# Eight shared PSUM banks, diagonal score blocks of their own, and two copies moved to ScalarE

## The chip, the core and the metric

The kernel runs on one core of a Trainium2 chip. The metric is the device time of one execution in microseconds (us), the median of several runs. The engines are named as the profile names them: PE (TensorE, the matmuls), PEld (its weight loads), DVE (VectorE), ACT (ScalarE), POOL (GpSimd) and SP (SyncE, which issues most transfers).

## What is computed

Attention over 4 batches of 8 heads, 768 positions of 64 values each, in which every query sees only the six chunks of 32 keys with the highest upper bound; then a gated linear unit with a causal convolution of five taps over the 512 channels.

```python
k_min, k_max = min and max of k over each chunk of 32 keys
ub  = sum_d max(q * k_min, q * k_max)            # per query and chunk, causal chunks only
sel = the 6 chunks with the highest ub
scores = q @ k.T / 8, masked to sel and to key <= query
attn_out = softmax(scores) @ v                   # 4 x 8 x 768 x 64 -> x: 4 x 768 x 512
gate = sigmoid(sum_{k<5} conv_w[k] * x[t - 4 + k])
out  = (gate * (x @ w_val)) @ w_out              # 4 x 768 x 512, float32
```

## The kernel before, in words

Two heads of one batch make a pair; there are 16 pairs, four to a batch. For each pair `kq` (L423) transposes k and q on PE (L432), copies them out of PSUM on ACT (L443, L465, L470), reduces the chunk extremes on DVE (L449) and casts k, q and v to 16 bits on POOL (L457, L476, L496). `sel` (L501) computes the bounds by ten small fp32 matmuls of 48 columns (L509), of which each shows two records, takes the best six chunks on DVE (L515 to L530), transposes the resulting penalties on PE (L539) and copies them into rows of `QU` by two DVE copies of 24x640 (L545), so that the score matmul adds the penalty by itself.

`attn` (L563) computes the scores transposed (keys in partitions, queries in columns). A head has six key tiles of 128; key tile j meets the queries from 128j on, 2,688 columns in all. `banks` (L552) packs these columns into five PSUM banks of 512 per head, and `LAST` (L561) holds the last tile of both heads, so a pair has eleven banks: matmul (L580), exp on ACT (L587), and where a bank holds a block on the diagonal, a causal mask on POOL (L596, an affine select in place). Seven of the eleven banks have such blocks, 112 masks in all. Then 42 matmuls of 65 columns per pair (L613) multiply the probabilities by v into one accumulator bank per head; DVE divides by the sums (L624, L628), PE transposes (L637), and DVE copies 128x768 into `xT` (L642).

`moe_gate` (L646) runs two taps on PE (L656) and three on DVE (L664, L672), then tanh on ACT (L677). When a batch's four pairs are done, `moe_val` (L681) and `moe_out` (L700) run its two dense products (L687, L703), with DVE (L694) and ACT (L708) behind them.

What sets the order: nothing is written out by hand. Each operation is added to a `Plan` with an engine, a key (its due time, in pairs) and a cost. `Plan.order` (L78) is a list scheduler: it walks a model of the engines, takes for each engine among the operations that could start soonest the one with the lowest key, and the kernel is emitted in that order, each engine in its own queue. A matmul of kind "u" (L509) gets a lower key behind a long matmul, so that its two weight loads run beside that. Where the model sees PE idle, `fill` (L137) puts in matmuls of zeros (L414), hosted by an open accumulator bank.

PSUM has eight banks of 512 columns. Three pools hold them: tag "w" (transposes, bounds, gate, val, out), "s" (scores), "av" (accumulators), with fixed counts; a new tile takes the oldest of its own pool:

```python
    BUFS = {"w": 3, "s": 3, "av": 2, "kn": 3, "qn": 3, "vn": 3, "P5": 2, "kmx": 2, "kmr": 2,
```

Of the kernel before, what the change touches and what calls it, by code (L numbers as in the profile page):

```python
# [16 lines left out]
class Op:  # L17
    __slots__ = ("eng", "key", "cost", "fn", "kind", "reads", "writes", "new", "need", "ndep",
                 "outs", "after", "ready", "end", "num", "what")


class Plan:
# [7 lines left out]

    def __init__(self):
        self.ops = []
        self.writer = {}
        self.readers = {}
        self.maker = {}

    def add(self, eng, key, cost, fn, r=(), w=(), new=(), kind=None, what="", at=0.0):
        o = Op()
        o.eng, o.key, o.cost, o.fn, o.kind, o.new, o.what = eng, key, cost, fn, kind, new, what
        o.reads, o.writes = tuple(r), tuple(w)  # L40
        o.outs, o.ready, o.end, o.num = [], at, None, len(self.ops)
        need = set()
        for x in o.reads:
            if x in self.writer:
                need.update(self.writer[x])
            self.readers.setdefault(x, []).append(o)
        for x in o.writes:
            need.update(self.readers.get(x, ()))
            if x in self.writer:
                need.update(self.writer[x])  # L50
# [6 lines left out]
        o.after = []  # L57
        for name, _ in new:
            self.maker[name] = o
        for x in o.reads + o.writes:  # L60
            d = self.maker.get(x)
            if d is not None and d is not o and d not in need:
                d.after.append(o)
                o.ndep += 1
# [3 lines left out]
    def also(self, names):  # L68

        o = self.ops[-1]  # L70
        o.reads += names
# [6 lines left out]
    def order(self, bufs, banked, filler):  # L78
# [3 lines left out]
        made, users, bank = {}, {}, {}  # L82
        tags = {name: tag for o in self.ops for name, tag in o.new}
        hosts, work = [], []
        for o in self.ops:
            for x in set(o.reads + o.writes + tuple(n for n, _ in o.new)):
# [3 lines left out]
        wait = {e: [] for e in engs}  # L90
        for o in self.ops:
            if o.ndep == 0:
                wait[o.eng].append(o)
        pe = dict(ldw=0.0, mm=0.0, kind=None)
        dma = 0.0
        done = []

        def clear(o, name):

            mine = set(users[name])  # L100
            for u in users[name]:
                makers = [self.maker[x] for x in u.reads if x in self.maker]
                for d in list(u.need) + makers:
# [5 lines left out]

        def slot(o):  # L110
            t = 0.0
            for name, tag in o.new:
                if tag == "w" and not clear(o, name):
                    return None
                row = made.setdefault(tag, [])
                if len(row) >= bufs[tag]:
                    for u in users[row[len(row) - bufs[tag]]]:
                        if u.end is None:
# [692 lines left out]
```

## Time and profile before

| | |
|---|---|
| median of 3 runs | 239.38 us (239.34 to 239.44) |
| the profiled execution | 240.22 us, of which the span of its instructions is 238.2 us |
| busy, share of the span | PE 88%, PEld 65%, DVE 79%, ACT 64%, POOL 61% |
| mean granted TensorE clock | 0.971 of full speed |
| by stage | 0 to 15 us start-up; 15 to 215 us the pairs; 215 to 238.2 us the last pair's end and the last batch's products |

Busy time is time in which an engine worked on an instruction; the ends of matmuls are modelled, so a PE that is busy need not issue at its full rate. Durations of neighbouring ACT or DVE instructions overlap a little, so that a group's busy time can be below its count times its mean. "Idle before" and "waited for" name what ended an engine's idle time. The chain is the work that ended last, followed back from the end.

### The profile page before, as it was taken

The page shows a single profiled execution, that of the slowest core. Times are in us where ns is not written, and L with a number is a line of the kernel's source. Part 1 is how long each engine was busy: PE and PEld are TensorE (multiplying, and loading weights), DVE is VectorE, ACT ScalarE, POOL GpSimd, SP SyncE. Part 2 cuts the span into 40 slices and gives each one's busy share as a digit, 9 for nine tenths or more (in the row PEclk, how much of TensorE's full clock was granted, in tenths as well). Part 3 has the DMA queues.
Part 4 walks back from the last instruction along what each step waited for, and adds up shares of the span by engine and source line. Part 5 has one row for each costly group of instructions (what it writes and reads, how often), then busy time and mean ns, then how long its engine had stood idle before and what let it go on. Part 6 is the DMA issues. An engine that isn't in the chain of part 4 may idle for free.

```text
span 238.2 us, 5674 instructions
## 1 busy us (share of the span) xinstructions
PE 210.7 (88%) x2028; PEld 155.1 (65%) x2028; DVE 188.6 (79%) x542; ACT 152.1 (64%) x313; POOL 144.9 (61%) x288
## 2 busy tenths in 40 slices
PE   7978789878889988799899999999999998998893
PEld 2565668755858856675768676858686776754541
DVE  4349994968599999769597999998989799867750
ACT  2317838267859467557869767559878578396143
POOL 2399956978988546647775938676838677133000
PEclk9999959979999999799999999999999999999999
DMA  8999999853549033316757625335121000023115
GB/s 156 224 218 219 202 185 192 149 131 88 127 105 221 12 69 91 78 32 133 203 147 185 135 66 119 82 69 154 47 91 48 0 3 0 3 94 126 47 45 219
DMA packets 80201, 26.87 MB, mean 113 GB/s; under 512 B 75738, under 2 KB 77102, under 8 KB 80174
## 3 DMA queue, kind: packets, MB, share of 16 engines
q1 hardware_dynamic: 77182, 24.79, 46.4%
q0 software_dynamic: 1056, 1.05, 3.1%
q10 hardware_dynamic: 1936, 0.68, 1.5%
q8 instruction: 16, 0.26, 0.5%
q14 instruction: 11, 0.09, 0.1%
HBM read 21.27 MB, written 6.29 MB: 116 GB/s over the span
## 4 chain that ended last, share of the span: by engine, by line
PE 40%; DVE 30%; POOL 14%; ACT 7%; issue 5%; DMA 1%; POOLq 1%; ACTq 0%; DVEq 0%
PE t_w L509 7%; POOL t_P L596 6%; PE t_s L580 5%; PE t_av L613 5%; PE t_w L656 5%; POOL QU L476 4%; PE t_w L703 4%; ACT t_P L587 4%; PE t_w L432 4%; PE t_av L414 4%; PE t_w L687 4%; DVE t_g L664 4%; POOL KE L457 3%; DVE t_g L672 3%; DVE t_top L523 3%
## 5 line engine op out<-in xcount | busy, mean ns | idle before, releaser
L587 ACT ACTIVATE t_P<-t_s 128x512 f16<-128x512 f32 (+1 forms) x176 | 92.3, 592 | 25.2 <-PE t_s L580 24.7
L596 POOL TENSOR_SCALAR_AFFINE_SELECT t_P<-t_P 128x256 f16<-128x256 f16 (+1 forms) x112 | 51.4, 467 | 42.2 <-ACT t_P L587 39.5
L580 PE MATMUL t_s<-QU,KE 88*128 88x512 f16 (+7 forms) x256 | 60.2, 312 | 2.0 <-DMA t_kn<-in_k_dram 0.5
L613 PE MATMUL t_av<-VA,t_P 128*128 128x65 f16 x672 | 43.7, 196 | 9.8 <-POOL t_P L596 7.7
L613 PEld LDWEIGHTS <-t_P 128*128 128x128 f16 x672 | 37.1, 103 | 22.3 <-POOL t_P L596 14.0
L457 POOL CAST KE<-t_k 64x384 f16<-64x384 f32 x64 | 35.8, 560 | 19.3 <-ACT t_k L443 15.7
L476 POOL CAST QU<-t_q 64x384 f16<-64x384 f32 x64 | 36.3, 567 | 4.5 <-ACT t_q L465 2.0
L443 ACT ACTIVATE t_k<-t_w 128x384 f32<-128x384 f32 x32 | 15.8, 498 | 28.9 <-PE t_w L432 27.0
L672 DVE SCALAR_TENSOR_TENSOR t_g<-xT,cwT,t_g 128x768 f32<-128x768 f16 x32 | 33.8, 1057 | 0.3
L509 PEld LDWEIGHTS t_w<-KB,t_rq 128*128 128x128 f32 x160 | 27.8, 194 | 7.1 <-DVE KB L489 2.3
L687 PE MATMUL t_w<-xT,wval_sb 128*128 128x384 f16 x128 | 29.9, 331 | 1.3 <-DVE t_gv L694 1.3
L509 PE MATMUL t_w<-KB,t_rq 128*128 128x48 f32 x160 | 27.6, 255 | 3.5 <-DVE KB L489 3.5
L509 PEld LDWEIGHTS t_w<-KB,t_q 128*128 128x128 f32 x160 | 28.0, 194 | 1.4 <-issue 0.6
L580 PEld LDWEIGHTS <-KE 88*128 88x128 f16 (+1 forms) x256 | 23.3, 107 | 8.2 <-issue 3.8
L656 PE MATMUL t_w<-xT,diag 128*128 128x384 f16 x128 | 27.9, 330 | 0.7 <-DVE t_g L664 0.4
L509 PE MATMUL t_w<-KB,t_q 128*128 128x48 f32 x160 | 27.4, 253 | 0.0
L703 PE MATMUL t_w<-wout_sb,t_gv 128*128 128x512 f16 x96 | 26.9, 379 | 0.1
L449 DVE TENSOR_REDUCE t_kmx<-t_k 128x12 f32<-128x384 f32 x32 | 17.3, 541 | 8.3 <-ACT t_k L443 8.3
L664 DVE SCALAR_TENSOR_TENSOR t_g<-xT,cwT,t_w 128x384 f32<-128x384 f16 x32 | 19.4, 607 | 5.4 <-PE t_w L656 4.7
L708 ACT ACTIVATE t_osb<-t_w 128x512 f32<-128x512 f32 x24 | 14.5, 603 | 11.1 <-PE t_w L703 8.3
L496 POOL CAST VA<-t_vn 128x384 f16<-128x384 f32 x32 | 16.6, 527 | 7.4 <-PE t_av L613 4.3
L432 PE MATMUL t_w<-ident,t_qn 128*128 128x128 f32 x96 | 17.5, 286 | 2.8 <-DVE t_mub L515 2.2
(49 smaller groups left out, 318.2 us busy)
## 6 DMA issues: line engine op xcount, KB each, us to landing
t_vn<-in_v_dram SPq DMA_DIRECT2D x32, 192.0 KB, 4.0
out_dram<-t_osb SPq DMA_DIRECT2D x24, 256.0 KB, 2.0
t_kn<-in_k_dram SPq DMA_DIRECT2D x31, 192.0 KB, 3.6
t_qn<-in_q_dram SPq DMA_DIRECT2D x31, 192.0 KB, 4.2
wval_sb<-in_moe_w_val_dram POOLq DMA_DIRECT2D x1, 512.0 KB, 7.2
wout_sb<-in_moe_w_out_dram POOLq DMA_DIRECT2D x1, 512.0 KB, 7.7
t_kn<-in_k_dram ACTq DMA_DIRECT2D x1, 192.0 KB, 4.2
t_qn<-in_q_dram ACTq DMA_DIRECT2D x1, 192.0 KB, 5.5
```

Source lines behind the costliest of these rows:

```text
L457: pool(k0 + (0.6 if p else 2.5), 0.56, lambda hh=hh: nc.gpsimd.tensor_copy(out=ke[HP[hh], hh, sl], in_=T["k32", p][HP[hh], sl]), r=(("k32" ...
L476: pool(k0 + 0.3, 0.56, lambda hh=hh: nc.gpsimd.tensor_copy(out=qu[HP[hh], hh, sl], in_=T["q32", p][HP[hh], sl]), r=(("q32", p, w), ("q32", ...
L509: pe(key, 48, lambda it=it, ts=ts, j=j, x=x: nc.tensor.matmul(out=T[pu][:, it - 1, :], lhsT=T[x, p][:, ts], rhs=kb[:, j, :], start=(j == 0 ...
L580: pe(kk, m, lambda hh=hh, c=c, jt=jt, q0=q0, m=m, bank=bank: nc.tensor.matmul(out=T[bank][:, c:c + m], lhsT=ke[KP[hh], hh, jt * 128:(jt + ...
L587: nc.scalar.activation(out=T[pt][:, 0:width], in_=T[bank][:, 0:width], func=AF.Exp, scale=0.125),
L596: nc.gpsimd.affine_select(out=ap, in_=ap, pattern=[[0, nt], [1, 128]], compare_op=ALU.is_ge, fill=0.0, base=0, channel_multiplier=-1)
L613: sp_=sp_: nc.tensor.matmul(out=T[pav][:, qt * 65:(qt + 1) * 65], lhsT=T[pt][:, col:col + 128], rhs=va[:, hh, jt, :], start=st, stop=sp_, ...
L656: nc.tensor.matmul(out=T[pg], lhsT=diag[:, ki * NCT + ct, part, :], rhs=xT[:, slot, w * HB + ki:w * HB + ki + HB], start=(n == 0), stop=(n ...
L664: dve(key + 0.1 * w, 0.55, lambda w=w, pg=pg, i=i: nc.vector.scalar_tensor_tensor(out=T[g][:, w * HB:(w + 1) * HB], in0=xT[:, slot, w * HB ...
L672: dve(key + 0.2, 1.0, lambda i=i, ki=ki: nc.vector.scalar_tensor_tensor(out=T[g], in0=xT[:, slot, ki:ki + S], scalar=cwT[:, i:i + 1], in1= ...
L687: pe(key + 0.05 * w, HB, lambda ct=ct, w=w, pv=pv: nc.tensor.matmul(out=T[pv], lhsT=wval_sb[:, ct, et * 128:(et + 1) * 128], rhs=xT[:, slo ...
L703: pe(key, DM, lambda et=et: nc.tensor.matmul(out=T[po], lhsT=T["gv", b, et][:, s * 128:(s + 1) * 128], rhs=wout_sb[:, et, :], start=(et == ...
```

## The change

Eight tiles `PB`, one per bank, are allocated once. A tile with tag "w", "s", "av" or the new "spare" no longer belongs to a pool: at the moment the scheduler places its first matmul, `bank_of` takes the bank, of all eight, that comes free first, as long as the tag stays under its cap (4, 4, 2, 1). The warm-up matmuls get the tag "spare". Costs of several operations in the scheduler's model are set anew, its matmul model is put into one function, and three kinds of transposes no longer count as PE activity.

The score columns are cut anew. `square(hh)` holds the four diagonal blocks of 128x128 of key tiles 0 to 3 of a head, `LAST` the two diagonal blocks of tiles 4 and 5 of both heads, and `banks` four banks with nothing on the diagonal. A pair still has eleven banks; three of them are masked, each by one mask of 128x512. The masked banks come first in `seq`, and the 65-column matmuls on them get a later key (0.25 pairs behind the scores, others 0.17).

Two copies change engine: the copy into `xT`, and one of the two penalty copies of a pair (`MASKS`), go from DVE to ACT.

```diff
+    NBANK = 8
...
+        def bank_of(tag):
+
+            same, best = [], None
+            for i, n in enumerate(banks):
+                t = 0.0 if n is None else over(n)
+                if n is not None and tags[n] == tag:
+                    same.append(t)
+                if t is not None and (best is None or t < best[0]):
+                    best = (t, i)
+            if best is None:
+                return None
+            lim = 0.0
+            if len(same) >= caps[tag]:
+                known = sorted(x for x in same if x is not None)
+                k = len(same) - caps[tag]
+                if len(known) <= k:
+                    return None
+                lim = known[k]
+            return max(best[0], lim), best[1]
+
         def slot(o):
             t = 0.0
             for name, tag in o.new:
-                if tag == "w" and not clear(o, name):
-                    return None
-                row = made.setdefault(tag, [])
+                if tag in caps:
+                    got = bank_of(tag)
+                    if got is None or tag == "w" and not clear(o, name):
+                        return None
+                    t = max(t, got[0])
+                    continue
...
-                o.end = s + o.cost + (0.16 if e != "POOL" else 0.1)
-                m = s
+                o.end = s + o.cost + {"ACT": 0.18, "DVE": 0.14, "POOL": 0.09}[e]
...
+    MASKS = ("DVE", "ACT")
...
-    BUFS = {"w": 3, "s": 3, "av": 2, "kn": 3, "qn": 3, "vn": 3, "P5": 2, "kmx": 2, "kmr": 2,
+    CAPS = {"w": 4, "s": 4, "av": 2, "spare": 1}
+    BUFS = {"kn": 3, "qn": 3, "vn": 3, "P5": 2, "kmx": 2, "kmr": 2,
...
+    PB = [ps.tile([128, 512], FP, tag=f"bank{i}", name=f"bank{i}") for i in range(Plan.NBANK)]
...
+        def mask(key, hh, fn, r, w):
+            if MASKS[hh] == "ACT":
+                act(key, 0.58, lambda: fn(copy=nc.scalar.copy), r, w)
+            else:
+                dve(key, 0.48, lambda: fn(copy=nc.vector.tensor_copy), r, w)
+
         for hh in range(2):
-            dve(key + 0.35, 0.43, lambda hh=hh: nc.vector.tensor_copy(
+            mask(key + 0.35, hh, lambda hh=hh, copy=None: copy(
                 out=qu[CP[hh], hh, 128:S], in_=T[pt][CP[hh], :]),
...
+    def square(hh):
+        return [(hh, 128 * j, j, 128 * j, 128) for j in range(4)], 4
+
     def banks(hh):
         return [
-            ([(hh, 0, 0, 256, 512)], ()),
-            ([(hh, 0, 0, 0, 256), (hh, 256, 4, 512, 256)], (0, 256)),
-            ([(hh, 0, 1, 256, 512)], ()),
-            ([(hh, 0, 1, 128, 128), (hh, 128, 3, 384, 384)], (0, 128)),
-            ([(hh, 0, 2, 256, 512)], (0,)),
+            ([(hh, 0, 0, 128, 512)], 0),
+            ([(hh, 0, 0, 640, 128), (hh, 128, 2, 384, 384)], 0),
+            ([(hh, 0, 1, 256, 512)], 0),
+            ([(hh, 0, 3, 512, 256), (hh, 256, 4, 640, 128)], 0),
         ]
 
-    LAST = ([(0, 0, 5, 640, 128), (1, 128, 5, 640, 128)], (0, 128))
+    LAST = ([(hh, 256 * hh + 128 * j, 4 + j, 512 + 128 * j, 128) for hh in range(2)
+             for j in range(2)], 4)
...
-        seq = [(b0[j], f"P0{j}") for j in range(5)] + [(LAST, "P5")]
-        seq += [(b1[j], f"P1{j}") for j in range(5)]
+        seq = [(square(0), "P04"), (LAST, "P5")] + [(b0[j], f"P0{j}") for j in range(4)]
+        seq += [(square(1), "P14")] + [(b1[j], f"P1{j}") for j in range(4)]
...
-                pool(kk, 0.38 if nt > 1 else 0.28, tri, r=(pt,), w=((pt, "tri"),))
+                pool(kk, 0.62, tri, r=(pt,), w=((pt, "tri"),))
...
-                    pe(kk + 0.17, 65, lambda pav=pav, pt=pt, qt=qt, col=col, hh=hh, jt=jt, st=st,
+                    pe(kk + (0.25 if tris else 0.17), 65, lambda pav=pav, pt=pt, qt=qt, col=col, hh=hh, jt=jt, st=st,
...
-        dve(key + 1.15, 0.48, lambda: nc.vector.tensor_copy(out=xT[:, slot, 4:4 + S], in_=T[pt]),
+        act(key + 1.15, 0.66, lambda: nc.scalar.copy(out=xT[:, slot, 4:4 + S], in_=T[pt]),
```

How the instructions stand on POOL in the middle of the program, around one pair's attention, before (`t_P` are the probabilities, `KE`, `QU`, `VA` the casts for later pairs):

```order
L596 AFFINE_SELECT t_P_1927<-t_P_1927 128x2x128
L596 AFFINE_SELECT t_P_1966<-t_P_1966 128x256
L457 CAST KE_76<-t_k_1977 64x384
L596 AFFINE_SELECT t_P_1983<-t_P_1983 128x128
L457 CAST KE_76<-t_k_1977 64x384
L596 AFFINE_SELECT t_P_2008<-t_P_2008 128x256
L596 AFFINE_SELECT t_P_2026<-t_P_2026 128x2x128
L457 CAST KE_76<-t_k_1977 64x384 x2
L596 AFFINE_SELECT t_P_2062<-t_P_2062 128x256
L596 AFFINE_SELECT t_P_2072<-t_P_2072 128x128
```

And in the changed kernel, there too:

```order
L648 AFFINE_SELECT t_P_1545<-t_P_1545 128x512
L648 AFFINE_SELECT t_P_1552<-t_P_1552 128x512
L502 CAST KE_78<-t_k_1601 64x384 x4
L521 CAST QU_81<-t_q_1670 64x384 x2
L648 AFFINE_SELECT t_P_1690<-t_P_1690 128x512
L541 CAST VA_82<-t_vn 128x6x64
```

The seven masks of a pair, spread between the casts, have become three: two at the start of a pair's attention and one at the second head's.

On DVE one pair's stretch before, with both penalty copies (L545, into `QU`) and the copy into `xT` (L642):

```order
L642 COPY xT<-t_w 128x768
L523 MAX t_top_2264<-t_mub 128x8 x6
L624 RECIPROCAL t_rcp<-t_av 128x6
L530 TENSOR_TENSOR NS_88<-t_mub,t_top_2264 128x10x24
L449 TENSOR_REDUCE t_kmx<-t_k_2227 128x12
L664 SCALAR_TENSOR_TENSOR t_g_2334<-xT,cwT,t_w 128x384
L449 TENSOR_REDUCE t_kmr<-t_k_2227 128x12
L545 COPY QU_79<-t_w 24x640
L482 TENSOR_TENSOR t_kmr<-t_kmx,t_kmr 128x24
L664 SCALAR_TENSOR_TENSOR t_g_2334<-xT,cwT,t_w 128x384
L489 TENSOR_TENSOR KB_85<-t_kmr 64x2x24 x2
L545 COPY QU_79<-t_w 24x640
```

On ACT in the changed kernel, one pair's stretch (L641 is the exp, L694 the copy into `xT`, L596 the penalty copy, L488, L510 and L515 the copies of k and q, L760 an output copy):

```order
L694 COPY xT<-bank_91 128x768
L641 ACTIVATE t_P_2043<-bank_90 128x512
L760 ACTIVATE t_osb<-bank_94 128x512
L488 ACTIVATE t_k_2060<-bank_96 128x384
L641 ACTIVATE t_P_2069<-bank_89 128x512
L488 ACTIVATE t_k_2060<-bank_94 128x384
L641 ACTIVATE t_P_2099<-bank_95 128x384
L510 ACTIVATE t_q_2113<-bank_96 128x384
L515 ACTIVATE t_rq<-bank_96 128x256
L641 ACTIVATE t_P_2131<-bank_91 128x512
L641 ACTIVATE t_P_2142<-bank_89 128x512
L596 COPY QU_79<-bank_96 24x640
```

The two copies now stand between exps of a pair, in the queue that the exps go through.

## Rows read from the trace of the kernel before

**Rows 1.** The page: busy us, share of the span of 238.2 us, instructions.
```profile
PE 210.7 (88%) x2028; PEld 155.1 (65%) x2028; DVE 188.6 (79%) x542; ACT 152.1 (64%) x313; POOL 144.9 (61%) x288
```

**Rows 2.** Stage: us, PE, PEld, DVE, ACT, POOL busy, granted clock, DMA share, GB/s.
```profile
15.00:215.00 200.00, 181.80 (x1867) 140.35 (x1866) 170.57 (x504) 140.07 (x292) 136.75 (x269) 0.97 0.50 108
```

**Rows 3.** The chain that ended last, by engine.
```profile
PE 40%; DVE 30%; POOL 14%; ACT 7%; issue 5%; DMA 1%; POOLq 1%; ACTq 0%; DVEq 0%
```

**Rows 4.** Waits: us in total, times, longest us.
```profile
PEld L613 <- POOL t_P L596: 14.0, 22, 2.0
PE t_av L613 <- POOL t_P L596: 7.7, 14, 1.6
PE t_w L509 <- DVE KB L489: 3.5, 5, 1.5
PE t_w L432 <- DVE t_mub L515: 2.2, 1, 2.2
...
PE t_w L539 <- DVE t_g L664: 0.2, 1, 0.2
```

**Rows 5.** Groups by shape: count, busy us, mean ns; idle before and releaser.
```profile
L587 ACT ACTIVATE t_P<-t_s 128x512 f16<-128x512 f32 x160 | 88.0, 612 | 21.8 <-PE t_s L580 21.3
L596 POOL TENSOR_SCALAR_AFFINE_SELECT t_P<-t_P 128x256 f16<-128x256 f16 x80 | 40.1, 503 | 36.4 <-ACT t_P L587 34.7
L545 DVE COPY QU<-t_w 24x640 f16<-24x640 f16 x32 | 15.5, 483 | 0.9
L677 ACT ACTIVATE t_g<-t_g 128x768 f32<-128x768 f32 x16 | 13.5, 845 | 8.8 <-DVE t_g L672 8.4
L596 POOL TENSOR_SCALAR_AFFINE_SELECT t_P<-t_P 128x128 f16<-128x128 f16 x32 | 12.0, 375 | 5.7 <-ACT t_P L587 4.8
L642 DVE COPY xT<-t_w 128x768 f16<-128x768 f16 x16 | 8.8, 551 | 8.3 <-PE t_w L637 5.7 <-PE t_av L613 2.6
```

**Rows 6.** Timeline, 94.9 to 96.2 us: a mask beside a DVE instruction.
```profile
94.90 1.00 DVE L672 SCALAR_TENSOR_TENSOR t_g<-xT,cwT,t_g 128x768 f32<-128x768 f16 x1
94.90 1.27 POOL L596 TENSOR_SCALAR_AFFINE_SELECT t_P<-t_P 128x256 f16<-128x256 f16 x1
96.23 0.30 PE L613 MATMUL t_av<-VA,t_P 128*128 128x65 f16 x4 [1.61 <-POOL t_P L596]
```

**Rows 7.** Busy time in three stretches of half clock; columns as in Rows 2.
```profile
30.00:36.60 6.60, 5.94 (x43) 4.36 (x44) 6.02 (x25) 2.98 (x6) 3.25 (x6) 0.50 1.09 184
50.30:53.70 3.40, 3.40 (x24) 2.72 (x22) 1.69 (x5) 1.83 (x5) 1.86 (x6) 0.50 0.95 215
98.10:101.50 3.40, 3.40 (x27) 3.40 (x26) 1.53 (x4) 0.69 (x2) 1.47 (x5) 0.50 0.38 86
```

**Rows 8.** Timeline of PE before the second of these stretches.
```profile
49.66 0.42 PE L613 MATMUL t_av<-VA,t_P 128*128 128x65 f16 x8 [1.37 <-POOL t_P L596]
```

**Rows 9.** Timeline of PE: spacing of matmuls, alone and mixed.
```profile
13.32 0.39 PE L509 MATMUL t_w<-KB,t_rq 128*128 128x48 f32 x2 [1.55 <-DVE KB L489]
13.55 0.39 PE L509 MATMUL t_w<-KB,t_q 128*128 128x48 f32 x2
...
42.16 0.32 PE L509 MATMUL t_w<-KB,t_rq 128*128 128x48 f32 x2
42.31 0.33 PE L656 MATMUL t_w<-xT,diag 128*128 128x384 f16 x1
...
116.58 0.50 PE L637 MATMUL t_w<-identh,t_onat 128*128 128x128 f16 x6
...
228.77 5.34 PE L703 MATMUL t_w<-wout_sb,t_gv 128*128 128x512 f16 x24
```

**Rows 10.** Tile t_w: count, ns of one matmul, lowest/median/highest; first and last start.
```profile
L637 PE MATMUL t_w<-identh,t_onat x96: 216/219/311, 37.9 to 220.5; 128*128 128x128 f16 x96
L703 PE MATMUL t_w<-wout_sb,t_gv x96: 376/379/381, 109.4 to 233.7; 128*128 128x512 f16 x96
```

**Rows 11.** Timeline, the end: the last copy into xT.
```profile
220.75 0.56 DVE L642 COPY xT<-t_w 128x768 f16<-128x768 f16 x1 [0.60 <-PE t_w L637]
```

More of the change, by code (lines that the diff above doesn't have):

```diff
@@ L18 @@
     __slots__ = ("eng", "key", "cost", "fn", "kind", "reads", "writes", "new", "need", "ndep",
[L19 removed]
+                 "outs", "after", "ready", "end", "num", "seen")
 class Plan:
+    NBANK = 8
     def __init__(self):
@@ L56, in add, with behind @@
             d.outs.append(o)
-        o.after = []
         for name, _ in new:
             self.maker[name] = o
[L60 to L64, printed above, removed]
+        self.behind(o, o.reads + o.writes)
         self.ops.append(o)
         return o
-    def also(self, names):
-        o = self.ops[-1]
-        o.reads += names
+    def behind(self, o, names):
         for x in names:
@@ L76, in also, with order @@
                 o.ndep += 1
[L78 to L84, printed above, removed]
+    def also(self, names):
+        o = self.ops[-1]
+        o.reads += names
+        self.behind(o, names)
+    def order(self, bufs, caps, filler):
+        users, tags, used = {}, {}, {}
+        made = {}
+        banks = [None] * self.NBANK
+        self.place = {}
+        hosts, work, done = [], [], []
         for o in self.ops:
+            tags.update(o.new)
             for x in set(o.reads + o.writes + tuple(n for n, _ in o.new)):
@@ L89, in order, with over @@
         free = dict.fromkeys(engs, 0.0)
[L90 to L93, printed above, removed]
+        wait = {e: [o for o in self.ops if o.eng == e and o.ndep == 0] for e in engs}
+        last_pe = {n: [u for u in users[n] if u.eng == "PE"][-1] for n in tags
+                   if tags[n] in caps and n in users}
         pe = dict(ldw=0.0, mm=0.0, kind=None)
         dma = 0.0
-        done = []
+        def over(name):
+            t = 0.0
+            for u in users[name]:
+                if u.end is None:
+                    return None
+                t = max(t, u.end)
+            return t
         def clear(o, name):
@@ L101, in clear @@
             for u in users[name]:
-                makers = [self.maker[x] for x in u.reads if x in self.maker]
-                for d in list(u.need) + makers:
+                for d in list(u.need) + [self.maker[x] for x in u.reads if x in self.maker]:
                     if d not in mine and d.end is None:
@@ L196, in order @@
             for name, tag in o.new:
[L197 to L222 removed]
+                if tag in caps:
+                    i = bank_of(tag)[1]
+                    if banks[i] in hosts:
+                        hosts.remove(banks[i])
+                    banks[i] = name
+                    self.place[name] = i
+                    used[name] = {}
+                    if tag in ("av", "spare"):
+                        hosts.append(name)
+                else:
+                    made.setdefault(tag, []).append(name)
+            if e == "PE":
+                s = matmul(o, s)
             elif e in ("SP", "ACTQ"):
```

164 lines of the change are left out of this document (78 added, 86 removed).

## Prediction

> **What bounds the kernel now.** I read the page first, then the stages, the chain, the waits, and last the timeline at the places that these name. No engine is full: PE is busy 88% of the span, DVE 79%, ACT 64%, POOL 61% [rows 1]. In the 200 us in which the pairs run, PE is busy 181.80, DVE 170.57, ACT 140.07, POOL 136.75 [rows 2], so PE idles 18.2 us there. The chain passes through PE for 40% of the span, DVE 30%, POOL 14% and ACT only 7% [rows 3]. So the time is set by PE's order and by the moments at which PE waits. Who ends those waits is in the list of waits [rows 4]: the masks on POOL cost PE 7.7 us in 14 waits (14.0 us in 22 waits by its weight loads), and DVE costs it 10.4 us in eleven rows, of which the first two and the last stand there. About half of these 10.4 us are not data but banks: a matmul that waits for DVE to have read the bank which it is to write (2.2 and 0.2 in the rows shown).
>
> The granted clock was half in three stretches, 13.4 us together, each at 0.50, so 1.2 GHz instead of 2.4 [rows 7]. Ahead of the first PE had made its one wait of 2.2 us for DVE's `t_mub` [rows 4], ahead of the second it waited 1.37 us for a mask [rows 8], ahead of the third 1.61 us for a mask [rows 6].
>
> **The sum** is made against the profiled execution, 240.22 us; the median of the runs is 0.84 us less, 239.38.
>
> **Masks: less 6.0 us.** 112 masks become 48. At their mean durations the old ones take 80 x 0.503 + 32 x 0.375 = 52.2 us; 128 columns more cost 0.128 us, so one of 512 columns should take 0.503 + 2 x 0.128 = 0.76 us [rows 5], 36.4 us for 48. POOL's 16 us are worth nothing by themselves, since POOL idles anyway; what counts is PE's 7.7 us. In proportion to their number, 64/112 of these go: 4.4. Of the other 3.3 I take half away too, 1.6, because the order puts more work between the scores of a masked bank and the first matmul on its probabilities: counting the columns that PE issues between them (an fp32 transpose four times), a tenth of the masked banks had 3,108 or fewer and the least 1,224; now a tenth has 4,043 or fewer and the least 3,104. Against the other half speaks that each mask is 0.26 us longer. The ends are 0 and 14.0. A mask's duration varies: one of 256 columns took 1.27 us while DVE ran an instruction with two SBUF inputs for 1.00 us beside it, against a mean of 0.503 [rows 5, 6]. The Trainium skill, SBUF — State Buffer, section Who interferes with whom, says that a DVE instruction with two SBUF inputs and a GpSimd instruction that reads SBUF hold one shared port pair in turn, each for its whole length, while a DVE instruction with at most one SBUF input outside the two-port modes doesn't contend. By it the copies moved here, which read PSUM, never held POOL up, and the 32 long instructions that did are all still there. The row agrees with that rule as far as one place can; what it would do to the time is a rival below.
>
> **Clock: less 1.7 us.** Work in 13.4 us at half rate is worth at most 6.7. Two of the stretches, 6.8 us, begin behind mask waits; they cost up to 3.4. With fewer and shorter waits PE idles less ahead of them; I take half. Ends: 0 and 6.7.
>
> **DVE and the banks: less 6.3 us.** DVE loses 16 copies of 0.55 us and 16 of its 32 of 0.485 [rows 5], 16.6 us. The chain puts 30% of 238.2, so 71.5 of DVE's 188.6 busy us, on the path: 38% [rows 1, 3]. 38% of 16.6 is 6.3. The ends are 0 and the 10.4 that PE waits for DVE; shared banks act on the same 10.4 us, so I don't count them a second time. That a score tile may now take a fourth bank, or a transpose one that the scores don't need, can also give PE work in places where the trace shows no wait but only a late order; this I can't price, and it is the main reason for the long lower side of the range.
>
> **ACT: plus 2.8 us.** It gets 16 copies of 128x768 and 16 of 640 columns. The nearest rows are 0.845 for a 768-column instruction and 0.61 for one of 512; between them 0.73 for 640 [rows 5]. 16 x (0.845 + 0.73) = 25.2 us. From below, the same copies took 16.6 on DVE. In the stage of the pairs ACT goes from 140 to about 164 of 200 us. ACT's share on the path is now 7% of 238.2, 16.7 of 152.1 busy us, 11%: 2.8 us. Queued behind such a copy stand exps, and behind those PE. Ends: 0 and 38% (what DVE has now), 9.6 us. The exps themselves cost the same: eleven banks and as many columns as before.
>
> **PE's own work: plus 1.8 us.** Score columns stay the same, but 256 score matmuls become 384. Six 128-column matmuls took 0.50 us from the first's start to the last's end and one takes 0.219, so they start 0.056 apart; 24 of 512 columns took 5.34 and one takes 0.379, so (5.34 - 0.379)/23 = 0.216 [rows 9, 10]. Four times 0.056 is 0.224: 0.008 for three more matmuls, 0.4 us for 128. The bound matmuls lose cover: alone they start 0.225 us apart, beside a long matmul one costs 0.15 [rows 9]. In the order, 118 of the 159 followers of a bound matmul had a long matmul between, now 99: 19 x 0.075 = 1.4 us. Ends: 0, and 4.8 if each of the 64 long score matmuls that are gone takes its cover along. The zero matmuls behind the start-up, 19 before and one now, stood in gaps and count nothing.
>
> **End: plus 0.3 us.** The last pair's copy into `xT` stands on the path, 0.56 us on DVE [rows 11]; on ACT 0.845 [rows 5]. The first stage, bound by loads, stays. Loads and stores are the same transfers.
>
> Sum: -6.0 - 1.7 - 6.3 + 2.8 + 1.8 + 0.3 = **-9.1 us**, so 231.1 for an execution like the profiled one and **230.3 us** for the median.
>
> **The rivals.**
> - *ACT becomes what PE waits for (slower).* Place: the queue between scores and probabilities, where each copy of 0.73 to 0.845 us stands ahead of an exp. If ACT has DVE's present share on the path, the copies cost 9.6 us; the bound matmuls' and the splits' 1.8 and the end's 0.3 stay, DVE's relief is worth nothing because DVE is no longer waited for, and the late exps eat what the masks save. That is 239.4 + 11.7 = 251 at worst; if the masks' 6.0 are kept, 245.1. It decides from ACT above some 170 of the 200 us, DVE's present load; I work out 164. For it: ACT is the one engine that gets work. Against it: 36 us of idle time remain, and ACT waits for PE in nearly all its idle time before exps, 21.3 of 21.8 [rows 5].
> - *The masks stay blocked.* Each of 48 long masks may meet one of the 32 instructions of 1.0 us and take up to 1.8; then PE waits as now, the clock falls as now, and the 6.0 and the 1.7 are gone: 239.4 - 1.4 = 238.0. This is what the rule on the port pair would make of it. For it the 1.27 us mask; against it the longer distance in the order.
> - *PE closes nearly all of its gaps.* Masks 7.7, DVE and banks 10.4, clock 6.7, less the added 4.9: 19.9, so 219.5. For it: 18.2 us of idle PE in the pairs and a freer choice of banks.
> - *No change.* The waits only move: PE idles as much behind other releasers, since every pair still runs through the same chain of bounds, selection, scores, exp and product. Then 239.4.
>
> **How the numbers follow.** A measurement of this kernel tells 0.2%, 0.5 us, from no change. The forecast has a chance of 0.55 (225 to 236 us), blocked masks 0.11, closed gaps 0.10, no change 0.08, ACT as the bound 0.16. Faster: 0.55 + 0.11 + 0.10 = 0.76; same 0.08; slower 0.16. The range goes from 219, which takes in the closed gaps, to 242, which takes in no change and a mild form of the ACT case; beyond it lie the rest of that case and a schedule better than any wait shown here.
>
> **What would show it.** Right: PE's waits for masks at 2 us or less instead of 7.7, masks of about 0.76 us; DVE about 155 and ACT about 164 busy us over a like stage of the pairs; PE idle there near 10 us; less than 10 us at half clock. Wrong: PE waits for exps (L641) or for copies on ACT by more than 5 us, ACT's share of the chain above 20%; mask durations above 1 us in the mean; or PE's idle time unchanged under other names.

## The result and the profile after

The changed kernel takes **217.94 us** (median of 4 runs, 217.11 to 220.47), the kernel before, timed beside it, 239.41 us (239.34 to 240.13): a ratio of 0.9086 [0.9052, 0.9119]. The gain is 21.5 us. I had forecast 9.1, and the time lies just under my range, which began at 219. The profiled execution took 218.06 us. Executions of one kernel differ in their granted clock (the kernel before took 235.2 to 236.1 us at 1.00 and 239.0 to 241.5 at 0.97 or less, in runs beside the experiments), so at a like clock some 18 us of the gain are left, and below a median is that of a kernel's faster group of runs where it had two, while the range takes in all runs.

The page of the changed kernel, its parts as in [rows 1] and [rows 3]: span, busy us by engine, the granted clock in 40 slices, the chain, and the groups of the masks and of the two moved copies (by shape).

```profile
span 216.3 us, 5883 instructions
PE 203.3 (94%) x2143; PEld 155.4 (72%) x2143; DVE 178.2 (82%) x510; ACT 168.8 (78%) x345; POOL 131.0 (61%) x224
PEclk9999969999999999999999999999999999999999
PE 55%; DVE 32%; ACT 7%; issue 3%; DMA 1%; ACTq 0%; DVEq 0%
...
L641 ACT ACTIVATE t_P<-bank 128x512 f16<-128x512 f32 x144 | 79.3, 608 | 4.2 <-PE bank L634 3.8
L648 POOL TENSOR_SCALAR_AFFINE_SELECT t_P<-t_P 128x512 f16<-128x512 f16 x48 | 32.7, 694 | 22.1 <-ACT t_P L641 21.7
L694 ACT COPY xT<-bank 128x768 f16<-128x768 f16 x16 | 12.8, 802 | 3.4 <-PE bank L689 3.1
L596 ACT COPY QU<-bank 24x640 f16<-24x640 f16 x16 | 10.9, 681 | 4.5 <-DVE QU L596 3.4 <-PE bank L584 0.5
```

PE is now busy 94% of a shorter span, POOL has left the chain, ACT is still at 7% of it although it works 16.7 us more, and one slice alone shows a clock below full.

The first and last copies into `xT` mark the same points of the work in every kernel here. Tile `xT`, in both kernels: count, ns lowest/median/highest, first and last start.

```profile
L642 DVE COPY xT<-t_w x16: 537/558/559, 38.5 to 220.8; 128x768 f16<-128x768 f16 x16
```

```profile
L694 ACT COPY xT<-bank x16: 798/798/822, 34.1 to 199.2; 128x768 f16<-128x768 f16 x16
```

Of 21.9 us of span, 4.4 are gained before the first copy, 17.2 between the first and the last, 0.3 behind it. The stages between these marks, before and then after (us, PE, PEld, DVE, ACT, POOL busy, clock, DMA share, GB/s):

```profile
15.00:38.50 23.50, 19.96 (x173) 15.07 (x172) 20.53 (x73) 15.50 (x35) 18.81 (x39) 0.85 1.18 207
38.50:220.80 182.30, 166.49 (x1741) 127.72 (x1740) 154.31 (x440) 128.27 (x265) 119.72 (x233) 0.98 0.40 95
```

```profile
15.00:34.10 19.10, 16.82 (x175) 14.57 (x175) 18.29 (x63) 13.93 (x31) 16.89 (x30) 0.91 1.16 213
34.10:199.20 165.10, 161.09 (x1842) 127.11 (x1841) 146.97 (x419) 146.19 (x301) 107.34 (x177) 1.00 0.47 108
```

Between the marks PE idled 15.8 us (182.30 - 166.49) and now idles 4.0. What is left of its waits, the largest of PE and the two largest of its weight loads for masks and exps (us, times, longest), where before stood [rows 4]:

```profile
PEld bank L554 <- ACT t_P L641: 4.1, 8, 0.9
PEld L665 <- POOL t_P L648: 3.1, 10, 0.5
PE bank L665 <- DVE t_mub L560: 1.8, 1, 1.8
PE bank L459 <- DVE junk L415: 1.3, 1, 1.3
PE bank L755 <- DVE t_gv L746: 0.9, 1, 0.9
PE bank L554 <- DVE KB L534: 0.8, 2, 0.5
```

PE's matmuls no longer wait for a mask at all; only their weight loads do, 3.1 us in place of 14.0, which can lie beside other matmuls. Leaving the start-up's `junk` out, PE waited 7.7 us for POOL, 10.4 for DVE and 2.1 for ACT; it now waits 0, 6.0 and 0.4.

So the accounts close. Of the 21.9 us of span, 13.8 are waits of PE (20.2 less 6.4). The clock gives 5.2: 0.029 x 238.2 = 6.9 us were lost to half rate, now 0.008 x 216.3 = 1.7. These 5.2 hold for this pair of executions only. The rest, 2.9, is 0.7 of idle time that the list names otherwise and 2.2 of busy time at full clock. A part of that is zero matmuls: there were 59, 14.8 us busy, and are 46, 13.4 us. For the remainder no line stands; the ends of matmuls are modelled, and I take it, without having shown it, that closer packing shortens their union.

That tells where the time went, not which edit took it. The experiments take the change apart: into the **cut** of the scores, the **copies**, the **banks**, and the **scheduler's numbers**, which my prediction had left unpriced.

### The profile page after: what moved, and what is told of

It is laid out like the page before. It is cut to its first block, busy times and chain, and to the rows that moved or that the text cites. A ratio compares the mean times of both kernels' runs of the same rounds, so it can differ in the third digit from the quotient of the medians.

```text
span 216.3 us, 5883 instructions
## 1 busy us (share of the span) xinstructions
PE 203.3 (94%) x2143; PEld 155.4 (72%) x2143; DVE 178.2 (82%) x510; ACT 168.8 (78%) x345; POOL 131.0 (61%) x224
## 4 chain that ended last, share of the span: by engine, by line
PE 55%; DVE 32%; ACT 7%; issue 3%; DMA 1%; ACTq 0%; DVEq 0%
PE bank L554 12%; PE bank L634 9%; PE bank L708 6%; PE bank L739 6%; PE bank L665 6%; DVE t_g L724 5%; PE bank L755 5%; PE bank L477 4%; DVE t_g L716 4%; PE bank L459 3%; DVE KB L534 3%; DVE t_kmx L494 3%; ACT t_P L641 3%; DVE t_kmr L494 3%; DVE t_top L568 3%
## 5 line engine op out<-in xcount | busy, mean ns | idle before, releaser
L641 ACT ACTIVATE t_P<-bank 128x512 f16<-128x512 f32 (+1 forms) x176 | 92.5, 589 | 6.2 <-PE bank L634 5.0
L634 PE MATMUL bank<-QU,KE 88*128 88x128 f16 (+7 forms) x384 | 63.7, 261 | 1.5 <-DVE QU L596 0.7
L665 PE MATMUL bank<-VA,t_P 128*128 128x65 f16 x672 | 44.3, 196 | 1.9 <-DVE t_mub L560 1.8
L648 POOL TENSOR_SCALAR_AFFINE_SELECT t_P<-t_P 128x512 f16<-128x512 f16 x48 | 32.7, 694 | 22.1 <-ACT t_P L641 21.7
L739 PE MATMUL bank<-xT,wval_sb 128*128 128x384 f16 x128 | 31.0, 325 | 0.2
L554 PE MATMUL bank<-KB,t_rq 128*128 128x48 f32 x160 | 28.6, 260 | 1.7 <-DVE KB L534 0.8
L755 PE MATMUL bank<-wout_sb,t_gv 128*128 128x512 f16 x96 | 27.0, 379 | 0.9 <-DVE t_gv L746 0.9
L554 PEld LDWEIGHTS bank<-KB,t_q 128*128 128x128 f32 x160 | 27.2, 193 | 0.6
L554 PE MATMUL bank<-KB,t_q 128*128 128x48 f32 x160 | 27.4, 253 | 0.0
L708 PE MATMUL bank<-xT,diag 128*128 128x384 f16 x128 | 27.2, 326 | 0.2 <-ACT xT L694 0.2
L488 ACT ACTIVATE t_k<-bank 128x384 f32<-128x384 f32 x32 | 15.6, 494 | 13.0 <-PE bank L477 11.1
```

The lines of the kernel that those rows point to most:

```text
L554: pe(key, 48, lambda it=it, ts=ts, j=j, x=x: nc.tensor.matmul(out=T[pu][:, it - 1, :], lhsT=T[x, p][:, ts], rhs=kb[:, j, :], start=(j == 0 ...
L634: pe(kk, m, lambda hh=hh, c=c, jt=jt, q0=q0, m=m, bank=bank: nc.tensor.matmul(out=T[bank][:, c:c + m], lhsT=ke[KP[hh], hh, jt * 128:(jt + ...
L641: nc.scalar.activation(out=T[pt][:, 0:width], in_=T[bank][:, 0:width], func=AF.Exp, scale=0.125),
L648: nc.gpsimd.affine_select(out=ap, in_=ap, pattern=[[0, tris], [1, 128]], compare_op=ALU.is_ge, fill=0.0, base=0, channel_multiplier=-1)
L665: sp_=sp_: nc.tensor.matmul(out=T[pav][:, qt * 65:(qt + 1) * 65], lhsT=T[pt][:, col:col + 128], rhs=va[:, hh, jt, :], start=st, stop=sp_, ...
L708: nc.tensor.matmul(out=T[pg], lhsT=diag[:, ki * NCT + ct, part, :], rhs=xT[:, slot, w * HB + ki:w * HB + ki + HB], start=(n == 0), stop=(n ...
```

## The experiments

Kernels that were timed together share their runs of the kernel before. All of them compute the whole result.

### One part undone at a time

Here the kernel before took 235.6 us (235.21 to 239.19). Counts of 3, 3, 2 in place of 4, 4, 2; the bank that comes free first is still taken of all eight:

```diff
-    CAPS = {"w": 4, "s": 4, "av": 2, "spare": 1}
+    CAPS = {"w": 3, "s": 3, "av": 2, "spare": 1}
```

> The changed kernel with fixed counts of banks again (caps 3, 3, 2 instead of 4, 4, 2). Theory B (shared banks give PE work where the trace showed only a late order): most of the 21.5 us comes back, 230 us or more, and PE idles 15 us or more between 15 us and the last pair. Theory M (the masks and the clock behind them): 220 us or less, PE's mask waits stay near 0. Theory D (DVE's relief): 220 us or less.

The old cut, seven masks to a pair (the columns of `banks` and `LAST` go back with it, as in the change):

```diff
...
-        seq = [(square(0), "P04"), (LAST, "P5")] + [(b0[j], f"P0{j}") for j in range(4)]
-        seq += [(square(1), "P14")] + [(b1[j], f"P1{j}") for j in range(4)]
+        seq = [(b0[j], f"P0{j}") for j in range(5)] + [(LAST, "P5")]
+        seq += [(b1[j], f"P1{j}") for j in range(5)]
...
-                pool(kk, 0.62, tri, r=(pt,), w=((pt, "tri"),))
+                pool(kk, 0.38 if nt > 1 else 0.28, tri, r=(pt,), w=((pt, "tri"),))
...
```

> The changed kernel with the old cut of the score columns: seven masks per pair again. Theory M: 228 us or more, PE waits for masks 7 us or more again and the clock falls to half for 10 us or more. Theory B: 222 us or less. Theory D: 222 us or less.

Both copies on DVE again:

```diff
-    MASKS = ("DVE", "ACT")
+    MASKS = ("DVE", "DVE")
...
-        act(key + 1.15, 0.66, lambda: nc.scalar.copy(out=xT[:, slot, 4:4 + S], in_=T[pt]),
+        dve(key + 1.15, 0.48, lambda: nc.vector.tensor_copy(out=xT[:, slot, 4:4 + S], in_=T[pt]),
```

> The changed kernel with both copies back on DVE. Theory D (DVE's 16.6 us were mostly on the path): 228 us or more, DVE busy above 190 us. Theories B and M: 220 to 223 us. If ACT were in the way of the exps (my term of plus 2.8), below 217.9.

The scheduler's old numbers: the time from an instruction's end to its reader's start, three costs of DVE instructions, and which transposes count as PE activity. Here the change takes out two kinds, the 16-bit transposes of the penalties and of the attention's output; the fp32 transposes didn't count in the kernel before either, so "three kinds" in the description of the change was one too many.

```diff
-            o.end = m + (398 + n) / 2400 + 0.05
+            o.end = m + (398 + n) / 2400 + 0.07
...
-                o.end = s + o.cost + {"ACT": 0.18, "DVE": 0.14, "POOL": 0.09}[e]
+                o.end = s + o.cost + (0.16 if e != "POOL" else 0.1)
...
-        dve(key + 0.1, 0.2, lambda: nc.vector.tensor_tensor(
+        dve(key + 0.1, 0.12, lambda: nc.vector.tensor_tensor(
...
-            dve(key + 0.1, 0.33, lambda hp=hp, c0=c0: nc.vector.tensor_tensor(
+            dve(key + 0.1, 0.22, lambda hp=hp, c0=c0: nc.vector.tensor_tensor(
...
-        dve(key, 0.39, lambda: nc.vector.tensor_tensor(
+        dve(key, 0.33, lambda: nc.vector.tensor_tensor(
...
-                new=new(pt, "w", [128, SELT * 128], F16) if i == 0 else (), kind="x")
+                new=new(pt, "w", [128, SELT * 128], F16) if i == 0 else ())
...
-                new=new(pt, "w", [128, S], F16) if qt == 0 else (), kind="x")
+                new=new(pt, "w", [128, S], F16) if qt == 0 else ())
```

> The changed kernel with the scheduler's old costs and end latencies and its old account of PE activity. Theory P (the order is better because its model is nearer to the chip): 224 us or more. Theories B, M and D: 217 to 221 us, with the same few waits of PE.

| undone | us (range) | ratio to before |
|---|---|---|
| larger counts | 225.03 (224.29 to 225.78) | 0.9539 [0.9434, 0.9644] |
| cut | 221.00 (220.89 to 221.24) | 0.9359 [0.9282, 0.9436] |
| copies | 218.57 (218.51 to 223.44) | 0.9289 [0.9150, 0.9429] |
| scheduler's numbers | 227.84 (227.64 to 229.40) | 0.9662 [0.9567, 0.9757] |

Against 217.8, the same median of the changed kernel, the counts are worth 7 us, the cut 3, the copies 1, the numbers 10 (some of it clock, which was 0.970 in all four runs without them). The old counts cost less than the theory of the banks had asked (230 or more); the choice among all eight banks stayed in that kernel, and is tested further below. The cut and the copies, on which most of my sum rested, matter least. Without the cut PE waits for masks again, and the time hardly moves. The waits and the chain of that kernel:

```profile
PE bank L664 <- POOL t_P L647: 5.6, 13, 0.7
...
PE 44%; POOL 30%; DVE 13%; ACT 6%; issue 5%; DMA 1%; POOLq 0%; ACTq 0%; DVEq 0%
```

POOL has 30% of that chain, and masks have 5.6 us of PE's time: more than the whole 3.1 us that the cut is worth there.

### Which of the scheduler's numbers

The kernel before took 240.07 us (238.49 to 241.26). The new numbers alone, in the kernel before (the last diff, read backwards):

> The kernel before, with nothing of the change but the scheduler's new costs, end latencies and account of PE activity. If the parts simply add (theory A: 9.9 us were lost without the costs): 229 to 230 us. If the new costs are only worth something with the new banks and the new cut (theory I, interaction): 236 us or more.

The changed kernel with one kind of old number each: the old end latencies, then the three old DVE costs, then the old account of PE's activity (each the lines of the last diff that it names, the matmul's `+ 0.07` with the latencies):

> The changed kernel with the old end latencies of the engines in the scheduler's model alone (0.16 and 0.1, matmul 0.07 us). Theory P1 (the order follows how soon the model thinks a result can be read): 224 us or more. Theory P2 (the three DVE costs decide): 219 us or less. Theory N (any change of the model's numbers reshuffles the order, and the time moves by some us either way): between 217 and 224 us without the three runs of parts adding up to 9.9 us.

> The changed kernel with the old costs of three DVE operations between the chunk extremes and the selection (0.12, 0.22, 0.33 us instead of 0.2, 0.33, 0.39; the rows of before show 0.257, 0.386, 0.399). Theory P2: 223 us or more, because bound matmuls are placed before their operands are ready and PE waits for KB and t_mub 5 us or more. Theory P1: 219 us or less. Theory N: as for the latencies.

> The changed kernel in which the two kinds of 16-bit transposes count as PE activity again, which decides where matmuls of zeros are put. Theories P1, P2: 217 to 219 us. If the clock's account were what the costs change: 221 us or more with over 10 us at half clock.

| kernel | us (range) | ratio to before |
|---|---|---|
| before, new numbers alone | 230.05 (229.87 to 238.63) | 0.9586 [0.9519, 0.9653] |
| changed, old latencies | 216.62 (215.60 to 217.81) | 0.9029 [0.8977, 0.9080] |
| changed, old DVE costs | 226.83 (226.38 to 229.32) | 0.9473 [0.9410, 0.9537] |
| changed, old account | 217.31 (217.06 to 217.87) | 0.9059 [0.9015, 0.9102] |

The first row flatters the numbers. The two runs behind its median had a clock of 1.00, the kernel before had 0.963 to 0.975 here; at a like clock the new numbers alone save 4.4 us (235.63 at 0.974 against 240.07 at 0.969).

In the changed kernel the three DVE costs carry it. They are those of the three steps ahead of and behind the bound matmuls: `t_kmr` (0.12, now 0.2), `KB` (0.22, now 0.33) and `t_mub` (0.33, now 0.39). The groups of these instructions by shape, in the kernel before (count, busy us, mean ns, idle before):

```profile
L489 DVE TENSOR_TENSOR KB<-t_kmr 64x48 f32<-64x48 f32 x32 | 12.4, 386 | 0.4
L515 DVE TENSOR_TENSOR t_mub<-t_w,cfill 128x240 f32<-128x240 f32 x16 | 6.4, 399 | 5.2 <-PE t_w L509 5.1
L482 DVE TENSOR_TENSOR t_kmr<-t_kmx,t_kmr 128x24 f32<-128x24 f32 x16 | 4.1, 257 | 0.2
```

They take 0.386, 0.399 and 0.257 us (in the changed kernel 0.454, 0.402 and 0.366). With the old numbers the scheduler places the bound matmuls where their operand isn't there yet. The waits of the changed kernel with the old DVE costs:

```profile
PE bank L554 <- DVE KB L534: 4.8, 8, 1.6
PE bank L665 <- DVE t_mub L560: 3.4, 1, 3.4
```

These two rows are 8.2 us against 2.6 in the changed kernel, 5.6 of the 9 us. In between and beyond:

```diff
-        dve(key + 0.1, 0.2, lambda: nc.vector.tensor_tensor(
+        dve(key + 0.1, 0.16, lambda: nc.vector.tensor_tensor(
...
-            dve(key + 0.1, 0.33, lambda hp=hp, c0=c0: nc.vector.tensor_tensor(
+            dve(key + 0.1, 0.275, lambda hp=hp, c0=c0: nc.vector.tensor_tensor(
...
-        dve(key, 0.39, lambda: nc.vector.tensor_tensor(
+        dve(key, 0.36, lambda: nc.vector.tensor_tensor(
```

> The three DVE costs half-way between old and new (0.16, 0.275, 0.36). Theory P2: between 220 and 225 us, PE waits for KB between the 0.8 and the 4.8 us at the ends. Theory N: anywhere between 215 and 228.

And costs as the rows have them, 0.26, 0.39 and 0.40:

> The three DVE costs at the durations that the rows of the trace show (0.26, 0.39, 0.40). Theory P2: 216 to 218 us, PE's waits for KB 1 us or less. Theory N: anywhere between 215 and 228.

Two edits without a meaning tell how much the order moves by itself: the scheduler's window of 0.04 us made 0.05, and the distance of the score banks' keys:

```diff
-                if s > lo + 0.04:
+                if s > lo + 0.05:
```

> The changed kernel with a change of the scheduler that means nothing: operations count as starting together within 0.05 instead of 0.04 us. Theory P2 (the three DVE costs act by their size): within 1.5 us of 217.9. Theory N (any change of numbers reshuffles the order and moves the time): off by 3 us or more, here or in the next.

```diff
-            kk = key + 0.085 * n
+            kk = key + 0.08 * n
```

> The changed kernel with the due times of a pair's eleven banks 0.08 instead of 0.085 pairs apart. Theory P2: within 1.5 us of 217.9. Theory N: off by 3 us or more.

Before took 240.15 us (238.62 to 240.82). Halfway costs: 220.72 (220.11 to 221.53), 0.9202 [0.9158, 0.9246]. Costs of the rows: 218.44 (218.01 to 218.82), 0.9110 [0.9066, 0.9154]. The two null edits: 220.27 (219.95 to 220.38), 0.9179 [0.9142, 0.9216], and 219.63 (218.44 to 221.03), 0.9157 [0.9102, 0.9211].

From old costs to the rows' costs the time goes 226.8, 220.7, 217.9, 218.4, and the wait for `KB` 4.8, 1.6, 0.8, 0.2: a dose with its response, of which the time shows only the first step clearly. For the null edits set the grain: with the old latencies and the old account, four such kernels lie between 216.6 and 220.3, and 220.7, 217.9 and 218.4 lie in or beside that stretch. The null edits are 2.4 and 1.7 us off the changed kernel, more than the 1.5 that I had allowed, less than the 3 of the theory that any change of numbers reshuffles. So 7 and 9 us are effects, and not of the clock: the old counts ran at 0.992, and one run with the old DVE costs took 226.57 at 0.990; the 3 of the cut and the 1 of the copies can't be told from another order of the same work.

### Parts alone, and in pairs

Before took 237.25 us (235.54 to 240.40); there is no interval of the ratio for these four. Shared banks and new numbers, with the old cut and both copies on DVE:

> The changed kernel with the old score cut and both copies on DVE: only the shared banks and the scheduler's new numbers are left. Theory Q (these two carry the gain; cut and copies stay within what edits that mean nothing do, 216.6 to 220.3): 223 us or less, although PE waits for masks 5 us or more. Theory A (the parts add: 3.1 for the cut and 1.9 for the copies): 222 to 224 us. Theory W (the cut and the copies are needed for the rest to work): 228 us or more.

The cut and the copies in the kernel before, without the rest:

> The kernel before with the new score cut and both copies on ACT, but with the old pools of banks and the old numbers of the scheduler. This is what my prediction priced at less 9.1 us. Theory A (7.1 and 9.0 us are missing): 233 to 236 us. Theory Q: 236 us or more. The forecast's own terms: 230 us, with PE's mask waits near 2 us.

Shared banks alone, with counts of 4, 4, 2:

> The shared banks with the old cut, the old copies and the old numbers of the scheduler. Theory A: 232 us. Theory Q: 228 to 233 us. If shared banks are of use only with a model near the chip: 236 us or more.

The cut alone:

> The kernel before with the new score cut alone. My term for the masks and the clock behind them: 6.0 + 1.7 us less, 231 to 233 us, PE's mask waits 2 us or less. Theory A: 236 us. Theory Q: 236 to 241 us, the mask waits gone and other waits of PE in their place.

| kernel | us (range) | PE waits for POOL, DVE, ACT, us |
|---|---|---|
| before | 237.25 (235.54 to 240.40) | 7.7, 10.4, 2.1 |
| the cut alone | 239.20 (238.76 to 244.38) | 6.0, 14.6, 3.0 |
| the cut and the copies | 241.28 (239.71 to 241.46) | 2.5, 14.9, 3.8 |
| banks alone | 219.57 (219.46 to 223.53) | 3.5, 7.3, 0 |
| banks and numbers | 215.50 (215.14 to 220.46) | 0.8, 5.1, 0.7 |

**Banks and numbers give the whole gain; on top of them the cut and the copies give none.** The banks alone, for which I had expected 228 us or more, give 18 us. One stretch, 15 to 195 us, in the kernel before, the changed one, banks and numbers, cut and copies (columns as above):

```profile
15.00:195.00 180.00, 163.20 (x1672) 127.06 (x1671) 154.77 (x463) 125.78 (x264) 128.11 (x251) 0.96 0.54 115
```

```profile
15.00:195.00 180.00, 173.95 (x1974) 139.55 (x1974) 161.67 (x474) 156.14 (x323) 123.59 (x205) 0.99 0.55 119
```

```profile
15.00:195.00 180.00, 173.81 (x1878) 136.24 (x1878) 168.19 (x505) 139.99 (x293) 133.79 (x269) 0.95 0.55 120
```

```profile
15.00:195.00 180.00, 162.24 (x1765) 132.02 (x1763) 144.91 (x423) 141.99 (x289) 115.50 (x194) 0.94 0.54 115
```

With banks and numbers DVE is the fuller, 168.19 of 180 us, and PE is as busy as in the changed kernel. With the cut and the copies DVE falls to 144.91, POOL to 115.50, and PE idles as long as before, 17.8 us against 16.8: a relief of both engines that buys PE nothing. How this kernel would compare at the clock of the kernel before isn't shown: it had 0.953 in all four runs, the other 0.968 to 1.00, and a few us of its 241.28 can be clock. Over the whole span PE idles 27.4 us in it and 27.5 in the kernel before. PE's waits in the kernel with the cut and the copies say why:

```profile
PE t_w L510 <- DVE KB L490: 3.4, 5, 1.5
PE t_w L540 <- DVE NS L531: 3.1, 2, 2.7
PE t_w L510 <- DVE t_gv L702: 2.7, 2, 2.2
PE t_av L621 <- POOL t_P L604: 2.5, 4, 1.2
PE t_s L590 <- ACT t_P L597: 2.2, 3, 1.9
PE t_w L695 <- DVE t_gv L702: 2.1, 5, 0.7
```

The waits for masks fall to 2.5 us, near the 2 that I had forecast. But PE then waits for `NS`, a step of the selection, and for `t_gv` twice, where a matmul waits for DVE to have read a bank. It was the rival "no change", the waits only move. And in the kernel with banks and numbers the masks, all 112 of them as before, cost PE this:

```profile
PE bank L664 <- POOL t_P L647: 0.8, 2, 0.5
```

I had expected at least 5 us there: a miss that says most. PE waits for the same masks, on the same engine, in one order and hardly in another.

### What the banks do

Two ways remain in which shared banks could act: a matmul waits for fewer releases, or the scheduler finds another order. The order of the kernel before, the same on every engine, with permanent tiles taken in turn within the old pools:

```diff
+    PB = [ps.tile([128, 512], FP, tag=f"bank{i}", name=f"bank{i}") for i in range(8)]
+    TURN = {"w": 0, "s": 0, "av": 0}
...
+            i = TURN[tag] % BUFS[tag]
+            TURN[tag] += 1
+            t = PB[{"w": 0, "s": 3, "av": 6}[tag] + i]
```

> The kernel before in exactly its own order on every engine; only the PSUM tiles are eight that stay, taken in turn within the old counts, so that a matmul into a bank waits for the readers of the columns it writes and no longer for the release of a pool's tile (515 waits attached on PE instead of 575). Theory O (the order is what counts): 238 to 240 us. Theory R (the release of pool tiles held PE up): 225 us or less, since shared banks alone gave 18 us.

Then the choice itself, with the old counts, the old cut, copies and numbers. Besides the choice only the warm-up's tag and the common matmul model, by which zero matmuls are now placed too, are left of what sets the order; these two weren't undone:

```diff
...
+                if t is not None and (best is None or t < best[0]):
+                    best = (t, i)
...
+    CAPS = {"w": 3, "s": 3, "av": 2, "spare": 1}
```

> Shared banks with the old counts (3, 3, 2) and with nothing else of the change: a tile takes whichever of the eight is free first, instead of the oldest of its pool. Shared banks alone with counts 4, 4, 2 gave 221.4. If the choice of the bank that is free first matters: 226 us or less. If the larger counts matter: 232 us or more.

Before took 238.00 us (235.59 to 241.45). Permanent tiles in the old order: 239.65 (237.25 to 240.66, ten runs), 1.0086 [1.0028, 1.0145]. PE has 515 waits on semaphores in its instructions instead of 575, and it is no faster, rather 0.9% slower. The bank that comes free first, at the old counts: 223.32 (221.36 to 223.64), 0.9381 [0.9294, 0.9468]. So 15 us come from the choice of a bank through the order that it allows, and none from fewer waits. The larger counts add 4 more when nothing else is changed (219.57), or 2 at a like clock of 0.99 (219.46 against 221.36), about the grain of the null edits; with all the rest of the change they are worth 7. The stage 38.5 to 200 us, before, tiles alone, and the bank that comes free first:

```profile
38.50:200.00 161.50, 147.75 (x1554) 115.36 (x1553) 139.12 (x401) 114.43 (x239) 112.70 (x220) 0.98 0.43 98
```

```profile
38.50:200.00 161.50, 147.66 (x1587) 114.82 (x1586) 142.09 (x407) 116.50 (x242) 113.81 (x223) 1.00 0.43 100
```

```profile
38.50:200.00 161.50, 154.45 (x1690) 119.81 (x1690) 148.51 (x434) 124.08 (x258) 119.69 (x230) 1.00 0.45 105
```

PE's idle time falls from 13.8 to 7.1 us by the choice and stays at 13.8 without it, though the clock of the second kernel is full too.

Why the choice helps is argued from the order, not isolated. A tile of the bounds lives long: ten matmuls fill it, and DVE reads it last. Under rotation the third tile of tag "w" after it has to wait for it, free banks or not. Counted in PE's order, at most two other "w" tiles were started while one of the bounds was open, in every pair of the kernel before; up to three with the choice alone, up to four in the changed kernel. I tried no kernel that lets only the bounds' bank be passed over.

## Why the prediction was right in direction and wrong in size

**The step that failed** is the sum's price for order. It gave the choice of a bank no term of its own ("shared banks act on the same 10.4 us, so I don't count them a second time") and the scheduler's numbers none at all; the runs give 15 us for the choice alone (223.32 against 238.00) and 9 to 10 for the numbers within the change. What the sum did price, masks 6.0 and DVE's relief 6.3, gains nothing that the runs show. So the direction was luck: the kernel is faster by the two edits without a term. The signs named for "right" came true all the same: no wait for masks, PE idle for 6 of 180 us, one short stretch at half clock. They couldn't tell shorter waits from a better order.

**What bounds the kernel: right.** PE's order and its waits set the time, no engine was full, and the gain came out of PE's idle time and, in the profiled pair, its clock.

**Masks, less 6.0: the waits went, for another reason.** All 7.7 us went, and a mask takes 0.694 us, not 0.76. But the proportion "64/112 of these go" fails. The cut alone leaves 6.0 of 7.7 us and saves nothing, cut and copies leave 2.5 and save nothing, and 112 masks in a better order cost 0.8. A wait at a mask wasn't the mask's price; other waits took its place as long as the order had no other work for PE.

**DVE and the banks, less 6.3: wrong edit, and capped in the wrong place.** DVE's waits fell by 4.4 us. DVE's relief, which I priced by its 38% of the chain, gives nothing that can be told from the grain (218.57 with the copies on DVE, 215.50 without cut and copies). DVE's busy time fell by 10.4 us (188.6 to 178.2), not by 16.6. The banks I let act "on the same 10.4 us" and didn't count again. The choice of a bank alone is worth 15 us, more than those 10.4: with it PE waits 5.2 us for POOL, 7.9 for DVE and 0 for ACT, so it took waits at masks and exps too. This is the step that failed by most. I named the better order as what I could not price, and then gave it no term.

**The scheduler's numbers: no term at all.** They are worth 4 us alone at a like clock, 9 to 10 in the changed kernel. The diff shows them, and the rows for `t_kmr`, `KB` and `t_mub` would have told that the old costs were 0.07 to 0.17 us too low. PE's 3.5 us at `KB` [rows 4] hung on that: with the new numbers alone no wait of PE for `KB` is left, while the masks still cost 8.4.

**Clock, less 1.7: too small for this pair.** It gave 5.2. I took half of two stretches. But the kernel before reaches 1.00 unchanged in some runs, and I took 0.5 us for the smallest difference that can be told, where its own runs spread over 6 us. The stretch that is left, here in the timeline of PE, begins just before 29.00 us, 1.7 us after the end of a wait for `t_mub` and during the first transposes behind a wait of 0.49 us for `NS`. The first of [rows 7] came sooner: it had begun by 30.00, before its wait for `t_mub` ended at 30.20.

```profile
27.29 0.29 PE L665 MATMUL bank<-VA,t_P 128*128 128x65 f16 x4 [1.78 <-DVE t_mub L560]
...
28.80 0.60 PE L584 MATMUL bank<-identh,NS 128*128 128x128 f16 x5 [0.49 <-DVE NS L575]
```

```profile
29.00:30.00 1.00, 1.00 (x19) 1.00 (x17) 0.97 (x5) 0.00 (x0) 0.91 (x3) 0.50 1.15 228
```

But the clock isn't what decides: banks and numbers ran in 217.4 us at a mean clock of 0.948, the lowest of the profiled executions.

**ACT, plus 2.8: harmless.** The copies cost 0.802 and 0.681 us, 23.7 in all, near the 25.2 that I worked out. PE's waits for ACT fell from 2.1 to 0.4 us and ACT's chain share stayed at 7%; only its weight loads wait longer for exps, 6.2 us against 3.8, and that doesn't reach the matmuls. Its load in 15 to 195 us, 156.14 of 180, is 87%, past the 85% (170 of 200) from which I had let the rival decide. Being full is not being late.

**PE's own work, plus 1.8, and the end, plus 0.3.** Busy time at full clock fell by 2.2 instead; the stage behind the last copy got 0.3 shorter, though that copy is 0.25 us longer.

**The rivals.** ACT as the bound and no change fell. Blocked masks fell as a price: single masks still take up to 1.40 us, with all 32 long DVE instructions there, but the mean is below the estimate and no matmul waits for one. "PE closes nearly all of its gaps" came nearest, at 219.5: it had 7.7, 10.4 and 6.7 less 4.9; the runs give 7.7, 4.4 and 5.2, another 1.7 from ACT's waits, and 2.2 on top in place of the 4.9. I gave it 0.10, because I asked which edit removes which wait; banks and numbers alone leave 6.6 us of these waits, the whole change 6.4.

**What stays open.** Whether it is the bounds' long-lived bank that rotation suffered from; why the counts are worth 7 us with the rest of the change and 2 to 4 without it; and how much of the clock belongs to a kernel and how much to an execution. The grain was measured on the changed kernel only. The kernel with banks and numbers alone (215.50) and the one with old latencies (216.62) can't be told from the change (217.94, or 219.6 and 220.3 with null edits).

## What to carry to other kernels

In a kernel that a list scheduler orders, a wait in the trace can be a place where the order ran out, and the edit that shortens the engine named there may only move the wait; test it alone before you price it. Look first at what forbids the scheduler an order (a rotation of buffers that holds free ones back) and at where its costs stand below the durations in the trace: the first shows in the code, the second in the rows, before any run. Make two edits without a meaning to learn the grain, here 216.6 to 220.3 us, before you credit a part with 2 or 3 us.

## What was not expected of the hardware

One mask of 128x512 took 0.694 us in the mean, less than 0.503 + 2 x 0.128 = 0.76 from the masks of 128 and 256 columns [rows 5]. Means of masks hold delays: the long ones have a median of 0.634 and go up to 1.397 us, the shorter ones go from 0.284 to 1.483, the 1.27 of [rows 6] among them. ACT's copy of 128x768 from PSUM took 0.802 us against DVE's 0.55, and it cost the kernel nothing that can be measured.
